# An RWKV-5 attention and SiLU feed-forward kernel: the first chunk's bonus term and state clearing move to ScalarE, and its y is finished one unit later

## The chip, the cores and the metric

The kernel runs on one core of a Trainium2 chip. Its engines are called as the profile calls them: PE (TensorE: matmuls; PEld is its weight load), DVE (VectorE), ACT (ScalarE), POOL (GpSimd) and SP (SyncE, which issues most DMAs). Each engine takes its instructions strictly in the order in which the program lists them, and waits at an instruction until all that it needs is there. The metric is the device time of one execution in microseconds (us), as the median of several runs.

## The reference

Four sequences of 768 tokens with 8 heads of 48 channels go through an RWKV-5 recurrence. Its result, 3072 tokens of 384 channels, goes through two matrices with a SiLU between them:

```
for t in range(768):
    cur   = outer(u * k[t], v[t])
    y[t]  = r[t] @ (state + cur)
    state = w * state + outer(k[t], v[t])
x   = y as (3072, 384)
h   = x @ w_in                      # 384 -> 2048
out = (h * sigmoid(h)) @ w_out      # 2048 -> 384
```

All inputs are float32. The state starts at zero.

## The kernel before

**Units.** Time is cut into 6 chunks of 128 tokens. A unit `i` is one chunk of one sequence: `divmod(i, 4)` gives chunk `sc` and sequence `b`, so units 0 to 3 are the first chunk of the four sequences, and there are 24. In a chunk the recurrence is written as matrix products: a masked 128x128 matrix A per head of decayed r and k times v (the part from inside the chunk), r times the state (the part from before; absent in chunk 0, where the state is zero), and the bonus term, which is the sum over channels of r\*u\*k, a number per token and head, times v.

**The steps of a unit** are small functions:
- `p1`: PE transposes r and k of the unit into PSUM (`tr`, `tk`); DVE multiplies them with the powers of the decay (`rT`, `kT`, lines 212 and 216). From unit 4 on ACT also makes a float16 copy of rT.
- `nat_v`: ACT casts v to float16. `nat_ku`, `nat_rk`: POOL computes k\*u and then r\*(k\*u). `nat_kc`: POOL computes k times the decay to the chunk's end (`kc`).
- `bonus_sum`: DVE sums r\*k\*u over the channels (`rku`, line 192). `bonus_vu`: POOL multiplies v by it (`vu`, line 198).
- `p2`: PE computes A of the even and odd heads (`ae`, `ao`, lines 226 and 228), DVE masks them to float16 (`am`, line 233).
- `p3y`: PE computes y from am, v and, from chunk 1 on, the state (lines 248, 251). `p3e`: DVE adds the bonus term and casts to float16 (`y16`, line 258).
- `p4`: PE transposes y16 (line 299), ACT copies it to SBUF (`xT`, line 300): the input of the feed-forward part.
- `sums`: PE computes the outer products of kc and v (line 267); `state`: DVE brings them into the state `st` and its float16 copy `st16` (lines 279, 281; 276 from chunk 1 on), and POOL scales the state for the next chunk (`sdec`).

The feed-forward part is cut into `l1(sc, ft)` (PE: x times 128 columns of `win`, line 311; ACT: SiLU, line 314) and `l2` (PE: times `wout`, line 323; DVE: copy out; SP: store). They stand in a list of fillers, from which `fill(n)` takes pieces to put between the steps of the attention part.

**Order.** The order of each engine is written out by hand. The program begins with the loads of six units on SP, constants, and a chain on DVE that builds the powers of the decay by doubling (`pi`, lines 148 to 152). Then comes the loop over units 0 to 3, in which no feed-forward work exists yet: there `spin(n)` issues n matmuls of zeros into a PSUM tile of its own. In round `s` the loop does p1, nat\_v, nat\_ku and nat\_rk of unit s, the bonus product, y, y16 and p4 of unit s-1, and p2 and bonus\_sum of unit s. Round 2 also issues the three loads of `win` on POOL's queue. After it come the loads of `wout` (POOL), k\*u and r\*k\*u of unit 4, kc of units 0 to 3, eight l1 for two sequences each, and p4 of unit 3 between them. Units 4 and 5 are then written out one step after another, with `sums` and `state` of units 0 to 5 among them; from unit 6 on there is a regular loop. A later load of a unit into one of the six input buffers waits until all who read the earlier unit there are done: for k that includes kc, for v it includes vu.

PSUM tiles share buffers by tag: `y` (two buffers) serves y, yT, sps, the row and column helpers and spin; `moe` (three) the l1 and l2 results and in the first loop tr and tk; `tA` (three) ae, ao and, later, tr and tk. A tile waits until its buffer is free.

Of the kernel before, what the change touches and what calls it, by code (L numbers as in the profile page):

```python
# [8 lines left out]
FP = mybir.dt.float32  # L9
F16 = mybir.dt.float16  # L10
AF = mybir.ActivationFunctionType
# [4 lines left out]
def kernel(  # L16
# [11 lines left out]
    nc = tc.nc  # L28

    B, H, S, D = r.shape  # L30
    C = 128
    NCH = S // C
    HD = H * D
    NP = H // 2
    PW = 2 * D
    PR = 64 + D
# [4 lines left out]
    NIN = 6  # L41
# [4 lines left out]
    wrk = ctx.enter_context(tc.tile_pool(name="wrk", bufs=2))  # L46
    ps = ctx.enter_context(tc.tile_pool(name="ps", bufs=1, space=bass.MemoryType.PSUM))
# [59 lines left out]
    nc.gpsimd.memset(pi[:, :, 0:1], 1.0)  # L107
    for i in range(NKC):
        nc.gpsimd.memset(kc[i][:, :, D:64], 0.0)
    for b in range(B):  # L110
        nc.gpsimd.memset(st[b], 0.0)
        nc.gpsimd.memset(st16[b], 0.0)
    for i in range(1, NIN):
        for t in (rin, kin):
            nc.vector.memset(t[i][:, :, D:64], 0.0)
    sil = cst.tile([128, 1], F16)
    nc.scalar.activation(out=sil, in_=junk[:, 0:1], func=AF.Silu)

    def spin(n):

        t = ps.tile([128, 512], FP, name="spin", tag="y", bufs=2)
        for _ in range(n):
            nc.tensor.matmul(t, junk[:, 0:128], junk, start=True, stop=True)

# [25 lines left out]
    n = 1  # L150
# [21 lines left out]
    def nat_ku(i):  # L172
        L = live.setdefault(i, {})
        L["ku"] = wrk.tile([128, H, D], FP, name="ku")
        nc.gpsimd.tensor_tensor(out=L["ku"], in0=kin[i % NIN][:, :, 0:D], in1=u_bc,  # L175
                                op=ALU.mult)

    def nat_rk(i):
        L = live[i]
        L["rku_f"] = wrk.tile([128, H, D], FP, name="rku_f")  # L180
        nc.gpsimd.tensor_tensor(out=L["rku_f"], in0=rin[i % NIN][:, :, 0:D], in1=L["ku"],  # L181
                                op=ALU.mult)

    def nat_kc(i):
        n = i % NIN
        nc.gpsimd.tensor_tensor(out=kc[i % NKC][:, :, 0:D], in0=kin[n][:, :, 0:D],  # L186
                                in1=lamC, op=ALU.mult)

    def bonus_sum(i):
        L = live[i]  # L190
        L["rku"] = wrk.tile([128, H], FP, name="rku")
        nc.vector.tensor_reduce(out=L["rku"], in_=L["rku_f"], axis=mybir.AxisListType.X,  # L192
                                op=ALU.add)

    def bonus_vu(i):
        L = live[i]
        L["vu"] = wrk.tile([128, H, D], FP, name="vu")
        nc.gpsimd.tensor_tensor(out=L["vu"], in0=vin[i % NIN],  # L198
                                in1=L["rku"].unsqueeze(2).broadcast_to([128, H, D]),
                                op=ALU.mult)  # L200

    def p1(i, tag="tA", mid=None):
        n = i % NIN
        L = live.setdefault(i, {})
        tr = ps.tile([128, NP, C], FP, name="tr", tag=tag, bufs=3)
        tk = ps.tile([128, NP, C], FP, name="tk", tag=tag, bufs=3)
        for t, src in ((tr, rin), (tk, kin)):
            flat = src[n].rearrange("p h d -> p (h d)")
            for p in range(NP):
                nc.tensor.transpose(t[0:PR, p, :], flat[:, 128 * p:128 * p + PR], ident)  # L210
        L["rT"] = wrk.tile([PR, NP, C], FP, name="rT")
        nc.vector.tensor_tensor(out=L["rT"], in0=tr[0:PR], in1=lamR, op=ALU.mult)  # L212
        if mid:
            mid()
        L["kT"] = wrk.tile([PR, NP, C], FP, name="kT")
        nc.vector.tensor_tensor(out=L["kT"], in0=tk[0:PR], in1=lamK, op=ALU.mult)  # L216
        if i >= B:
            L["rT16"] = wrk.tile([PR, NP, C], F16, name="rT16")
            nc.scalar.copy(out=L["rT16"], in_=L["rT"])  # L219

    def p2(i, between=None):
        L = live[i]
        ae = ps.tile([128, NP, C], FP, name="ae", tag="tA", bufs=3)
        ao = ps.tile([128, NP, C], FP, name="ao", tag="tA", bufs=3)
        for p in range(NP):
            nc.tensor.matmul(ae[:, p, :], L["kT"][0:D, p, :], L["rT"][0:D, p, :],  # L226
                             start=True, stop=True)
            nc.tensor.matmul(ao[:, p, :], L["kT"][64:PR, p, :], L["rT"][64:PR, p, :],  # L228
                             start=True, stop=True)
        L["am"] = []  # L230
        for a in (ae, ao):
            am = wrk.tile([128, NP, C], F16, name="am", bufs=4)
            nc.vector.tensor_tensor(out=am, in0=a,  # L233
                                    in1=maskM.unsqueeze(1).broadcast_to([128, NP, C]),
                                    op=ALU.mult)
            L["am"].append(am)
            if between:
                between()
                between = None

    def p3y(i):
        sc, b = unit(i)
        L = live[i]
        v16 = L["v16"]
        L["y"] = y = ps.tile([128, H, D], FP, name="y", tag="y", bufs=2)
        for p in range(NP):
            if sc:
                nc.tensor.matmul(y[:, 2 * p:2 * p + 2, :], L["rT16"][:, p, :],  # L248
                                 st16[b][:, p, :], start=True, stop=False)
            for j in range(2):  # L250
                nc.tensor.matmul(y[:, 2 * p + j, :], L["am"][j][:, p, :],  # L251
                                 v16[:, 2 * p + j, :], start=not sc,
                                 stop=(not sc or j == 1))

    def p3e(i):
        L = live[i]
        L["y16"] = wrk.tile([128, H, D], F16, name="y16")
        nc.vector.tensor_tensor(out=L["y16"], in0=L["y"], in1=L["vu"], op=ALU.add)  # L258
# [11 lines left out]
    def state(i):  # L270
        sc, b = unit(i)
        sps = live[i]["sps"]
        for p0, c0 in ((0, 0), (64, D)):
            dst = st[b][p0:p0 + D, :, c0:c0 + D]
            if sc:
                nc.vector.tensor_tensor(out=dst, in0=sps[p0:p0 + D, :, c0:c0 + D],
                                        in1=sdec[b][p0:p0 + D, :, c0:c0 + D], op=ALU.add)
            else:
                nc.vector.tensor_copy(out=st16[b][p0:p0 + D, :, c0:c0 + D],
                                      in_=sps[p0:p0 + D, :, c0:c0 + D])  # L280
                nc.vector.tensor_copy(out=dst, in_=sps[p0:p0 + D, :, c0:c0 + D])
        if sc:
            nc.gpsimd.tensor_copy(out=st16[b], in_=st[b])
        if sc < NCH - 2:
            nc.gpsimd.tensor_tensor(out=sdec[b], in0=st[b],
                                    in1=wCT.unsqueeze(2).broadcast_to([PR, NP, PW]),
                                    op=ALU.mult)
# [3 lines left out]
    def p4(i):  # L291
        sc, b = unit(i)
        L = live[i]
        if sc not in xts:
            xts[sc] = wrk.tile([128, NQ, B, C], F16, name="xT", bufs=3)
        yT = ps.tile([128, NQ, C], F16, name="yT", tag="y", bufs=2)
        yf = L["y16"].rearrange("p h d -> p (h d)")
        for q in range(NQ):
            nc.tensor.transpose(yT[:, q, :], yf[:, 128 * q:128 * q + 128], ident16)  # L299
        nc.scalar.copy(out=xts[sc][:, :, b, :], in_=yT)  # L300
# [48 lines left out]

    def to_cols_u():  # L350
        t = to_cols(urow)
        spin(1)
        to_rows(u_bc, lambda p: t[:, p:p + 1].broadcast_to([PR, 128]))

    for s in range(B):
        p1(s, tag="moe", mid=to_cols_u if s == 0 else None)
        nat_v(s)
        nat_ku(s)
        if s:
            bonus_vu(s - 1)  # L360
        nat_rk(s)
        if s == 2:
            for c0, c1 in ((0, 512), (512, 1024), (1024, 2048)):
                nc.gpsimd.dma_start(out=win[:, :, c0:c1],
                                    in_=moe_w_in[:, c0:c1]
                                    .rearrange("(q p) n -> p q n", p=128))
        if s:
            p3y(s - 1)
            p3e(s - 1)
        spin(3)  # L370
        p2(s)
        bonus_sum(s)
        spin(2)
        if s:
            p4(s - 1)
        if s == 1:
            to_rows(lamC, lambda p: lamCT[:, p, :])
        spin(2)
    bonus_vu(B - 1)
    p3y(B - 1)  # L380
    p3e(B - 1)
    nat_kc(0)
    for g in range(2):
        nc.gpsimd.dma_start(
            out=wout[:, 8 * g:8 * g + 8, :],
            in_=moe_w_out[1024 * g:1024 * g + 1024, :].rearrange("(f p) n -> p f n", p=128))
    a, b_ = B, B + 1
    nat_ku(a)
    nat_rk(a)
    for i in range(1, B):  # L390
        nat_kc(i)
    for ft in range(4):
        l1(0, ft, 0, 2)
    p4(B - 1)
# [12 lines left out]
    p1(a)  # L407
    fill(1)
    nat_v(a)
    bonus_sum(a)  # L410
    bonus_vu(a)
    sums(0)
    state(0)
    fill(1)
# [11 lines left out]
    sums(3)  # L426
    state(3)
    p1(b_)
    nat_ku(b_)
    nat_rk(b_)  # L430
    fill(1)
    p4(a)
    sums(a)
# [75 lines left out]
```

## Time and profile before

| | us |
|---|---|
| median of 10 runs | 219.46 (219.44 to 222.36) |
| profiled execution, its own time | 219.46 |
| its span, first to last instruction | 217.8 |
| PE busy | 207.0 |
| DVE busy | 118.5 |
| ACT busy | 92.7 |
| POOL busy | 118.9 |

The profile is one execution. Its span leaves out 1.66 us around the first and last instruction. PE is busy for 95% of it, but this counts the spin matmuls. The first l1 matmul starts at 26.15 us; the loop over units 0 to 3 runs before that. Idle time of an engine costs only where the engine that sets the end waits for it; the trace names, behind each wait, who ended it.

In timelines a line has the start and duration in us, the engine, the line of the kernel, the operation, what it writes and reads, its shape, a count and, in brackets, how long the engine was idle before it and what ended that. Several like instructions in a row stand as one line with their common duration. DMA runs at about 170 to 210 GB/s from 5 to 30 us and half of that in the middle of the kernel.

### The profile page before, as it was taken

Reading aid. Unit: us, or ns where it says so; the run is one execution under the profiler, and the core shown is the slowest. Engines: PE = TensorE matmul, PEld = TensorE weight load, DVE = VectorE, ACT = ScalarE, POOL = GpSimd, SP = SyncE. Lnnn points to the kernel's source line nnn. Section 1 sums busy time; section 2 is a strip of 40 time slices with the busy share of each in tenths; the row PEclk is TensorE's granted clock in tenths of the full one; section 3 lists DMA queues with packets and bytes.
Section 4 is the critical chain, followed back from the end, with each engine's and each line's share of the span. In section 5 each row is a group of like instructions: output and inputs, shape, how many; then the busy total and the mean of one; then the engine's idle time right before and its main releaser. Section 6 shows DMA issues by size and latency. Waiting matters only on the chain.

```text
span 217.8 us, 4605 instructions
## 1 busy us (share of the span) xinstructions
PE 207.0 (95%) x1781; PEld 137.3 (63%) x1781; DVE 118.5 (54%) x242; ACT 92.7 (43%) x192; POOL 118.9 (55%) x155
## 2 busy tenths in 40 slices
PE   7899988978999999999999999999999999999993
PEld 2566656557777787676567666567676557654561
DVE  6677749845385573586365467356466337520121
ACT  2403274556720572214783125782026772049400
POOL 8197699975744963948574675373475165200000
PEclk9999999999999999999999999999999999999999
DMA  4998999989943850738513465410210000110011
GB/s 93 206 210 171 191 197 186 194 176 192 188 92 89 186 107 3 180 81 178 108 39 73 116 140 123 93 39 2 75 38 36 3 0 22 55 72 0 3 72 72
DMA packets 81662, 22.32 MB, mean 103 GB/s; under 512 B 75368, under 2 KB 81256, under 8 KB 81640
## 3 DMA queue, kind: packets, MB, share of 16 engines
q1 hardware_dynamic: 78360, 18.88, 40.0%
q0 software_dynamic: 3280, 3.15, 9.0%
q8 instruction: 14, 0.23, 0.4%
q14 instruction: 8, 0.07, 0.1%
HBM read 20.45 MB, written 4.72 MB: 116 GB/s over the span
## 4 chain that ended last, share of the span: by engine, by line
PE 76%; POOL 6%; SPq 6%; DVE 5%; issue 2%; ACT 2%; DMA 2%; DVEq 0%; POOLq 0%
PE ops L323 29%; PE hps L311 24%; PE ae L226 9%; SPq L71 5%; PE tr L210 4%; PE tk L210 3%; PE sps L267 2%; DMA vin<-in_v_dram 2%; PE y L251 1%; PE yT L299 1%; PE y L248 1%; POOL rku_f L181 1%; DVE rT L212 1%; POOL vu L198 1%; DVE am L233 1%
## 5 line engine op out<-in xcount | busy, mean ns | idle before, releaser
L311 PE MATMUL hps<-xT,win 128*128 128x512 f16 (+1 forms) x348 | 70.5, 342 | 1.5 <-ACT gT L314 0.9
L323 PE MATMUL ops<-wout,gT 128*128 128x384 f16 x384 | 69.9, 326 | 0.0
L314 ACT ACTIVATE gT<-hps 128x512 f16<-128x512 f32 (+1 forms) x116 | 58.6, 524 | 24.0 <-PE hps L311 22.1
L198 POOL TENSOR_TENSOR vu<-vin,rku 128x384 f32<-128x384 f32 x24 | 19.9, 828 | 62.9 <-DVE rku L192 61.5
L323 PEld LDWEIGHTS <-gT 128*128 128x128 f16 x384 | 35.8, 98 | 21.3
L311 PEld LDWEIGHTS <-win 128*128 128x128 f16 x348 | 32.1, 98 | 24.1 <-issue 2.5
L233 DVE TENSOR_TENSOR am<-ae,maskM 128x512 f16<-128x512 f32 x24 | 16.6, 692 | 47.0 <-PE ao L228 47.0
L219 ACT CAST rT<-rT 112x512 f16<-112x512 f32 x20 | 12.4, 618 | 51.7 <-DVE rT L212 51.7
L327 DVE COPY osb<-ops 128x384 f32<-128x384 f32 x24 | 13.3, 556 | 33.2 <-PE ops L323 32.7
L226 PEld LDWEIGHTS ae<-rT,kT 48*128 48x128 f32 x192 | 23.1, 187 | 9.4 <-issue 6.7
L226 PE MATMUL ae<-rT,kT 48*128 48x128 f32 x192 | 27.7, 285 | 0.8 <-DVE kT L216 0.5
L228 PE MATMUL ao<-rT,kT 48*128 48x128 f32 x192 | 27.7, 285 | 0.0
L175 POOL TENSOR_TENSOR ku<-kin,u_bc 128x384 f32<-128x384 f32 x24 | 24.2, 1009 | 4.7 <-ACT u_bc L145 4.7
L181 POOL TENSOR_TENSOR rku_f<-rin,ku 128x384 f32<-128x384 f32 x24 | 24.0, 1001 | 1.6
L186 POOL TENSOR_TENSOR kc<-kin,lamC 128x384 f16<-128x384 f32 x24 | 23.9, 1000 | 0.0
L300 ACT COPY xT<-yT 128x384 f16<-128x384 f16 x24 | 11.4, 476 | 28.9 <-PE yT L299 28.9
L228 PEld LDWEIGHTS ao<-rT,kT 48*128 48x128 f32 x192 | 23.1, 187 | 0.0
L212 DVE TENSOR_TENSOR rT<-tr,pi 112x512 f32<-112x512 f32 x24 | 16.5, 689 | 9.0 <-PE tr L210 7.6
L233 DVE TENSOR_TENSOR am<-ao,maskM 128x512 f16<-128x512 f32 x24 | 16.4, 681 | 0.0
L216 DVE TENSOR_TENSOR kT<-tk,pi 112x512 f32<-112x512 f32 x24 | 16.3, 681 | 0.0
L258 DVE TENSOR_TENSOR y<-y,vu 128x384 f16<-128x384 f32 x24 | 13.3, 553 | 3.9 <-PE y L251 2.7
L210 PE MATMUL tr<-ident,rin 128*112 128x128 f32 x96 | 14.9, 279 | 0.0
(59 smaller groups left out, 208.8 us busy)
## 6 DMA issues: line engine op xcount, KB each, us to landing
rin<-in_r_dram SPq DMA_DIRECT2D x24, 192.0 KB, 4.0
kin<-in_k_dram SPq DMA_DIRECT2D x24, 192.0 KB, 3.6
vin<-in_v_dram SPq DMA_DIRECT2D x24, 192.0 KB, 3.6
out_dram<-osb SPq DMA_DIRECT2D x24, 192.0 KB, 1.9
wout<-in_moe_w_out_dram POOLq DMA_DIRECT2D x2, 768.0 KB, 12.5
win<-in_moe_w_in_dram POOLq DMA_DIRECT2D x2, 384.0 KB, 6.6
win<-in_moe_w_in_dram POOLq DMA_DIRECT2D x1, 768.0 KB, 10.0
wrow<-in_w_dram SPq DMA_DIRECT2D x1, 1.5 KB
```

Source lines behind the costliest of these rows:

```text
L175: nc.gpsimd.tensor_tensor(out=L["ku"], in0=kin[i % NIN][:, :, 0:D], in1=u_bc, op=ALU.mult)
L181: nc.gpsimd.tensor_tensor(out=L["rku_f"], in0=rin[i % NIN][:, :, 0:D], in1=L["ku"], op=ALU.mult)
L186: nc.gpsimd.tensor_tensor(out=kc[i % NKC][:, :, 0:D], in0=kin[n][:, :, 0:D], in1=lamC, op=ALU.mult)
L198: nc.gpsimd.tensor_tensor(out=L["vu"], in0=vin[i % NIN], in1=L["rku"].unsqueeze(2).broadcast_to([128, H, D]), op=ALU.mult)
L210: nc.tensor.transpose(t[0:PR, p, :], flat[:, 128 * p:128 * p + PR], ident)
L212: nc.vector.tensor_tensor(out=L["rT"], in0=tr[0:PR], in1=lamR, op=ALU.mult)
L226: nc.tensor.matmul(ae[:, p, :], L["kT"][0:D, p, :], L["rT"][0:D, p, :], start=True, stop=True)
L228: nc.tensor.matmul(ao[:, p, :], L["kT"][64:PR, p, :], L["rT"][64:PR, p, :], start=True, stop=True)
L233: nc.vector.tensor_tensor(out=am, in0=a, in1=maskM.unsqueeze(1).broadcast_to([128, NP, C]), op=ALU.mult)
L311: nc.tensor.matmul(hps, win[:, q, ft * 128:(ft + 1) * 128], xts[sc][:, q, b0:b1, :].rearrange("p b t -> p (b t)"), start=(q == 0), stop=(q ...
L314: nc.scalar.activation(out=gts[sc][:, ft, b0 * C:b1 * C], in_=hps, func=AF.Silu)
L323: nc.tensor.matmul(ops, gts[sc][:, ft, b * C:(b + 1) * C], wout[:, ft, :], start=(ft == 0), stop=(ft == NFT - 1))
```

## The change

Six edits, all for the units of the first chunk or for the steps just behind it:

1. POOL no longer zeroes the four states and their float16 copies at the start. A new function `clear` copies zeros with ACT, for states 0 and 1 at the end of round 0, for 2 and 3 at the end of round 1.
2. For units 0 to 3 the bonus product is made by ACT (`bonus_act`), one ACTIVATE per head with the sum as a scale per partition, in place of one POOL instruction. `rku` and `vu` get a third buffer.
3. Round s now does, of unit s-1, kc, bonus\_sum, the bonus product and y, and, of unit s-2, y16 (p3e) and p4. p3e stands ahead of p2 of the round. Round 3 also does bonus\_sum and the product of unit 3. y16 and p4 of units 2 and 3 follow the loop.
4. The spin matmuls write into the tile that the next real matmuls will fill (four ahead of the transposes, three ahead of ae), not into a tile of their own; `to_cols_u` has two in place of one. The rows of `lamC` are made in round 0, not in round 1.
5. In chunk 0 `state` makes the float16 copy on ACT; DVE keeps the float32 copy.
6. On POOL, k\*u and r\*k\*u of unit 5 and the bonus product of unit 4 stand ahead or beside the loads of `wout`; bonus\_sum(4) stands ahead of p1(4).

```diff
-    for b in range(B):
-        nc.gpsimd.memset(st[b], 0.0)
-        nc.gpsimd.memset(st16[b], 0.0)
...
+    def spin(n, t=None):
+        if t is None:
+            t = ps.tile([128, 512], FP, name="spin", tag="y", bufs=2)
+        else:
+            t = t.rearrange("s p t -> s (p t)")
...
+    def bonus_act(i):
+        L = live[i]
+        L["vu"] = wrk.tile([128, H, D], FP, name="vu", bufs=3)
+        for h in range(H):
+            nc.scalar.activation(out=L["vu"][:, h, :], in_=vin[i % NIN][:, h, :],
+                                 func=AF.Copy, scale=L["rku"][:, h:h + 1])
...
-    def p1(i, tag="tA", mid=None):
+    def p1(i, tag="tA", mid=None, spins=0):
...
+        spin(spins, tr)
...
-    def p2(i, between=None):
+    def p2(i, spins=0):
...
+        spin(spins, ae)
...
-                nc.vector.tensor_copy(out=st16[b][p0:p0 + D, :, c0:c0 + D],
-                                      in_=sps[p0:p0 + D, :, c0:c0 + D])
+                nc.scalar.copy(out=st16[b][p0:p0 + D, :, c0:c0 + D],
+                               in_=sps[p0:p0 + D, :, c0:c0 + D])
...
-        spin(1)
+        spin(2)
...
+    def clear(b):
+        zero = junk[0:PR, 0:HD].rearrange("r (p c) -> r p c", p=NP)
+        nc.scalar.copy(out=st[b], in_=zero)
+        nc.scalar.copy(out=st16[b], in_=zero)
+
     for s in range(B):
-        p1(s, tag="moe", mid=to_cols_u if s == 0 else None)
+        p1(s, tag="moe", mid=to_cols_u if s == 0 else None, spins=4 if s else 0)
         nat_v(s)
         nat_ku(s)
+        nat_rk(s)
         if s:
-            bonus_vu(s - 1)
-        nat_rk(s)
+            nat_kc(s - 1)
+            bonus_sum(s - 1)
+            bonus_act(s - 1)
+            p3y(s - 1)
+        if s == B - 1:
+            bonus_sum(s)
+            bonus_act(s)
         if s == 2:
             for c0, c1 in ((0, 512), (512, 1024), (1024, 2048)):
...
-        if s:
-            p3y(s - 1)
-            p3e(s - 1)
-        spin(3)
-        p2(s)
-        bonus_sum(s)
-        spin(2)
-        if s:
-            p4(s - 1)
-        if s == 1:
+        if s > 1:
+            p3e(s - 2)
+        p2(s, spins=3)
+        if s == 0:
             to_rows(lamC, lambda p: lamCT[:, p, :])
-        spin(2)
-    bonus_vu(B - 1)
+        if s > 1:
+            p4(s - 2)
+        if s < 2:
+            clear(2 * s)
+            clear(2 * s + 1)
+    p3e(B - 2)
     p3y(B - 1)
     p3e(B - 1)
-    nat_kc(0)
+    p4(B - 2)
+    a, b_ = B, B + 1
+    nat_ku(a)
+    nat_rk(a)
+    nat_kc(B - 1)
+    bonus_sum(a)
+    bonus_vu(a)
+    nat_ku(b_)
     for g in range(2):
...
-    a, b_ = B, B + 1
-    nat_ku(a)
-    nat_rk(a)
-    for i in range(1, B):
-        nat_kc(i)
+    nat_rk(b_)
...
-    bonus_sum(a)
-    bonus_vu(a)
...
-    nat_ku(b_)
-    nat_rk(b_)
```

More of the change, by code (lines that the diff above doesn't have):

```diff
@@ L117 @@
     nc.scalar.activation(out=sil, in_=junk[:, 0:1], func=AF.Silu)
-    def spin(n):
-        t = ps.tile([128, 512], FP, name="spin", tag="y", bufs=2)
+    def spin(n, t=None):
[3 more added lines that the diff above has]
+            t = t.rearrange("s p t -> s (p t)")
         for _ in range(n):
@@ L190, in bonus_sum @@
         L = live[i]
-        L["rku"] = wrk.tile([128, H], FP, name="rku")
+        L["rku"] = wrk.tile([128, H], FP, name="rku", bufs=3)
         nc.vector.tensor_reduce(out=L["rku"], in_=L["rku_f"], axis=mybir.AxisListType.X,
@@ L196, in bonus_vu @@
         L = live[i]
-        L["vu"] = wrk.tile([128, H, D], FP, name="vu")
+        L["vu"] = wrk.tile([128, H, D], FP, name="vu", bufs=3)
         nc.gpsimd.tensor_tensor(out=L["vu"], in0=vin[i % NIN],
@@ L200, in bonus_vu @@
                                 op=ALU.mult)
-    def p1(i, tag="tA", mid=None):
+    def bonus_act(i):
+        L = live[i]
+        L["vu"] = wrk.tile([128, H, D], FP, name="vu", bufs=3)
+        for h in range(H):
+            nc.scalar.activation(out=L["vu"][:, h, :], in_=vin[i % NIN][:, h, :],
+                                 func=AF.Copy, scale=L["rku"][:, h:h + 1])
+    def p1(i, tag="tA", mid=None, spins=0):
         n = i % NIN
@@ L236, in p2 @@
             L["am"].append(am)
-            if between:
-                between()
-                between = None
     def p3y(i):
```

## The prediction

> **What bounds the kernel now.** I read the page's busy shares first, then the table of windows, then TensorE's waits and timeline, and last the timelines of the other engines in the first 32 us. Shares, and four windows (us; busy time and instruction count of PE, PEld, DVE, ACT and POOL; granted clock; DMA share; GB/s):
>
> ```profile
> PE 207.0 (95%) x1781; PEld 137.3 (63%) x1781; DVE 118.5 (54%) x242; ACT 92.7 (43%) x192; POOL 118.9 (55%) x155
> ...
> 20.00:25.00 5.00, 4.88 (x53) 3.33 (x50) 3.88 (x7) 0.89 (x2) 4.38 (x6) 1.00 1.11 184
> 25.00:30.00 5.00, 3.99 (x40) 2.88 (x39) 1.92 (x4) 2.97 (x8) 3.55 (x5) 1.00 1.14 205
> 35.00:40.00 5.00, 4.04 (x44) 2.94 (x43) 4.85 (x15) 1.34 (x3) 4.56 (x6) 1.00 1.28 185
> 90.00:120.00 30.00, 30.00 (x271) 19.87 (x269) 17.57 (x34) 14.81 (x28) 19.24 (x24) 1.00 0.48 103
> ```
>
> From 60 to 200 us PE is full with work that the change leaves alone. So a microsecond won before 60 us comes off the end, and one lost is added. Up to 26 us PE looks busy, but much of that is spin matmuls; its first useful 256-column matmul (l1) starts at 26.15. After that it has short holes. From PE's timeline (start, duration, then in brackets the idle time before it and who ended it):
>
> ```profile
> 23.43 0.37 PE L226 MATMUL ae<-rT,kT 48*128 48x128 f32 x1
> ...
> 26.15 1.47 PE L311 MATMUL hps<-xT,win 128*128 128x256 f16 x12
> 27.92 0.34 PE L299 MATMUL yT<-ident,y 128*128 128x128 f16 x3 [0.30 <-DVE y L258]
> 28.83 1.36 PE L311 MATMUL hps<-xT,win 128*128 128x256 f16 x11 [0.57 <-ACT xT L300]
> 36.51 0.38 PE L267 MATMUL sps<-v,kc 128*112 128x96 f16 x4 [0.77 <-DVE st L281]
> 39.62 0.38 PE L267 MATMUL sps<-v,kc 128*112 128x96 f16 x4 [0.19 <-DVE st L281]
> 40.85 0.37 PE L226 MATMUL ae<-rT,kT 48*128 48x128 f32 x1 [0.21 <-DVE kT L216]
> 45.70 0.41 PE L267 MATMUL sps<-v,kc 128*112 128x96 f16 x4 [0.71 <-POOL kc L186]
> ```
>
> The question is therefore when that first l1, the second l1 group (28.83) and unit 5's ae (40.85) start afterwards. The rows that decide it, from the timelines of DVE, POOL and ACT:
>
> ```profile
> 3.99 1.60 DVE L148 COPY pi<-cols_sb 112x4 f32<-112x4 f32 x1
> 5.63 2.38 DVE L152 TENSOR_TENSOR pi<-pi 112x8 f32<-112x8 f32 x7
> ...
> 5.15 0.42 POOL L112 MEMSET stb<- 112x384 f16 x1
> 10.22 1.01 POOL L175 TENSOR_TENSOR ku<-kin,u_bc 128x384 f32<-128x384 f32 x1 [4.66 <-ACT u_bc L145]
> 19.14 2.47 POOL L364 DMA_DIRECT2D win<-in_moe_w_in_dram  x3
> ...
> 8.04 1.28 ACT L161 ACTIVATE lamCT<-pi 112x128 f32<-112x128 f32 x4 [5.74 <-DVE pi L152]
> ```
>
> **Zeroing leaves POOL.** Eight memsets go (2.66 to 5.57, 0.42 each). POOL has nothing to do then, so by themselves they are worth nothing. But the 112x4 copy L148 takes 1.60 us on DVE and ends 20 ns after the last memset, while an equal copy out of PSUM (L130) took 0.16. I take the memsets as its cause: the pi chain then ends at 6.6 instead of 8.0. The first rT moves from 8.15 to 6.9 (its transposes end at 6.85), kT from 8.82 to 8.0, because PE's u transposes at 7.63 set it, and u_bc's end from 10.14 to 9.35. The first ae comes at 9.4 instead of 10.20: 0.8 us earlier. If the copy stalls for another reason, this is 0. ACT pays with eight 112x384 copies at a pitch of 0.42 (v16: two in 0.93, one being 0.51), 1.7 us behind each of the first two units. That fits ACT's idle 5.33 us before 16.30.
>
> **Loop, units 0 to 2.** POOL does ku, rk, kc per unit (1.09 + 0.97 + 0.97, from pitches of those rows) instead of ku, vu, rk. Starting at 9.45 it ends kc(1) at 17.6. The three win triggers follow to 20.1 (19.14 to 21.61 before), then ku(3) and rk(3) to 22.15 (24.40 before). On DVE bonus_sum leaves its place between am and the next rT (0.46 of pitch, in the chain) for the place after kT, beside PE's 1.1 us of ae/ao. The chain per unit is then: ae/ao 1.1, am 1.3, transposes, rT and kT 1.3. The four spins ahead of the transposes hold the transposes back about as long as am takes (20.46 against 20.1 in unit 3), so putting spins inside awaited tiles is worth 0 to -0.4. By this count ae of units 1, 2, 3 starts at 13.8, 17.7, 21.8 (14.39, 19.23, 23.43 before): by unit 3 the loop is 1.6 us ahead. y16 was already beside ae/ao before (19.10, 23.48), so moving it gains nothing.
>
> **The bonus product on ACT.** One 0.83 us POOL instruction becomes eight ACTIVATEs of 128x48 with a pointer scale. No row has this shape. The nearest is lamCT (same function, pointer scale, 128 elements): four in 1.28 with 0.39 for one is a pitch of 0.297. The gT rows (0.598 for 512, 0.385 for 256) give 0.84 ns per element, so 48 elements are 0.23, and a product 1.85 us. Bounds: 0.12 (the 128x1 row, 0.21, less the overlap of 0.09) and 0.39 (no overlap). I take 0.23, nearest in kind.
>
> In units 1 and 2 this hides: product 0 runs 14.2 to 16.1, the zero copies of states 2 and 3 to 17.8, product 1 18.3 to 20.1, xT(0) to 20.5, and y(2) needs that PSUM buffer at 20.7. In unit 3 ACT must do two products in a row. rku(2) is ready at 22.2 and rku(3) at 22.7 (right behind POOL's rk(3)), so ACT is busy from 22.3 to 26.0, and xT(1) is queued behind: 26.0 to 26.45. On PE yT(2) waits for that PSUM buffer and l1 for xT(1), so the first l1 starts at 26.75, against 26.15: **0.6 later**, although its unit was 1.6 earlier. Behind it come xT(2), four gT (0.33 each) and xT(3), which ends at 29.2; the second l1 group starts at 29.25 against 28.83: **+0.4**. The 0.30 in front of yT(3) goes, and its gain is eaten by xT(3). bonus_sum(3) could hold am(3) behind it on DVE if POOL were late; by the count DVE is free at 22.15, just as rk(3) ends, and the cost is 0.2, included.
>
> **States 0 to 3 split over DVE and ACT.** DVE loses eight 48x192 copies (pitch 0.30), ACT gets them at about 0.32. kc(1) to kc(3), vu(4), ku(5) and rk(5) are now done on POOL before the first sums. Walking the same PE order from 29.25: sums(2) waits 0.3 instead of 0.77, sums(4) nothing instead of 0.19, and unit 5's kT is ready in time instead of 0.21 late; with the bonus_sum(4) ahead and the shorter DVE queue, ae(5) starts at 40.0, 0.85 ahead of 40.85. From the second l1 group to ae(5) it is then 10.75 us instead of 12.02: of these 1.27, 0.87 are the bracketed waits and 0.4 short gaps between PE's groups that carry no bracket. The 0.71 of kc(5) stays: am, rku, vu, kc follow ae(5) in the same order (4.85 us in both).
>
> **DMA.** win's triggers come 1.5 us earlier. Before, a piece took this long:
>
> ```profile
> DMA to landing us min/median/max: 6.1/7.1/10.0
> ```
>
> The first piece lands at 17.6 + 6.1 = 23.7. SP's loads of units 6 to 8 wait for kc and vu of units 0 to 2, so they now go out from about 19.7 instead of 28, and share the bus (about 190 GB/s). Sharing in halves would cost the 393 KB piece 2 us: 25.7, covered by PE's wait until 26.75; without that cover it adds its delay one for one. wout's triggers go from 28.17 to about 28.9 and are not needed before 57.
>
> **Sum.** +0.6 and +0.4 are one and the same delay seen twice, so: ae(5) 0.85 earlier, everything behind it unchanged, 219.46 - 0.85 = **218.6** (0.42 lost up to the second l1 group, 1.27 won behind it). The profiled execution's own time is 219.46 (span 217.8 and 1.66 around it), equal to the median.
>
> **Two rules of the skill.** PE's clock shows in the rows: four transposes took 1.06 us at 5.79 and 0.60 at 12.17. The Trainium skill (TensorE: Matmul & The Clock Gate, Part 1) says that an idle window of about 3.4 us halves the clock for the next one. By my count PE now has a hole from 23.4 to 26.5 with 0.2 us of work in it: under a window, so 0; if it fell in one, an estimate from that page is +1.7. The second: ScalarE: Activation LUTs, Rules for kernel authors, sends a multiplication to VectorE; its cost section (186 ns, 93 more for a pointer, 0.833 per element, 93 overlapped) gives 0.226 each, and the sum would still be 218.6.
>
> **Rivals.** *ACT is quick enough* (25%): at the low pitch of 0.12 xT(1) ends at 24.8, l1 starts at 25.5 behind y(3), the second group at 28.0: 217.3. For it: ACT was idle for 3.3 us of each unit before. Against: no row of ACT is that short. *No early start* (20%): the L148 stall is not POOL's; everything up to 26 us comes 0.8 later: 219.4, no change. Against it stands the 20 ns coincidence. *ACT's queue decides* (15%), the other side: a product is dearer than the count. At 0.297, as if length were free, three queued products push l1 to 27.8: 219.65; above about 0.29 the change no longer pays; at 0.39 product 1 also holds y(2) back, l1 starts at 30.35, and the time is 222.2. For it: 16 small instructions and xT(1) in one queue. *My forecast* holds 40%, 218.0 to 219.2.
>
> **How the numbers follow.** 0.5%, about what a measurement here can tell from no change, is 1.1 us: faster means below 218.36. Of my forecast a third lies there, of the quick ACT nearly all (0.13 + 0.24), and a little of the rest: 0.38. Slower (above 220.56) is most of the last rival: 0.14. Same is 0.48. The range runs from the quick ACT's 217.1 to 220.4, which leaves out the upper half of the ACT rival and a tail below.
>
> **What would show it.** Right: L148 near 0.15 us; first ae near 9.4 and fourth near 21.8; vu ACTIVATEs with a pitch of 0.23; a PE hole of about 3 us ahead of the first l1, ended by ACT xT; sums(2) waiting 0.3 or less. Wrong: L148 still 1.6; vu pitch of 0.3 or more; l1 ended by win's DMA; l2 or PE's transposes at half speed after 26 us.

## The result and the profile after

The changed kernel takes 221.08 us (median of 15 runs, 219.95 to 222.20) against 219.46 before. The ratio is 1.0059 with a 95% interval of 1.0037 to 1.0081: slower by about 0.6%, where 218.6 had been forecast. (The ratio and its interval are taken over all runs and not from the medians.) The single times fall into groups by the TensorE clock that the record of each run shows: 2 of 15 runs have a granted clock of 1.000 (219.95 and 220.09), 9 have 0.989 to 0.992 (about 221), 4 have 0.981 to 0.983 (about 222.1). The profiled execution is one of the middle group, 221.09 us with a span of 219.4.

First the table of windows of the changed kernel (columns as before: us, then busy time and count of PE, PEld, DVE, ACT and POOL, granted clock, DMA share, GB/s):

```profile
20.00:25.00 5.00, 3.01 (x41) 1.94 (x40) 4.22 (x8) 3.58 (x16) 4.84 (x6) 1.00 1.20 191
25.00:30.00 5.00, 3.60 (x21) 2.65 (x21) 1.02 (x2) 3.13 (x9) 3.83 (x5) 0.66 1.14 208
```

Two things differ from before. In 20 to 25 us PE was busy 4.88 us, now 3.01: the hole that the forecast expected. And the next row has a granted clock of 0.66, where every row of the kernel before had 1.00. The record of the clock gives its limits: half speed from 25.45 for 3.41 us, full speed from 28.86.

PE's timeline shows what that costs:

```profile
8.79 0.37 PE L235 MATMUL ae<-rT,kT 48*128 48x128 f32 x1
...
21.23 0.37 PE L235 MATMUL ae<-rT,kT 48*128 48x128 f32 x1
...
22.62 0.34 PE L305 MATMUL yT<-ident,y 128*128 128x128 f16 x3 [0.23 <-DVE y L264]
24.28 0.37 PE L257 MATMUL y<-v,am 128*128 128x48 f16 x8 [1.32 <-DVE y L264]
25.80 0.48 PE L305 MATMUL yT<-ident,y 128*128 128x128 f16 x3 [1.15 <-ACT xT L306]
26.07 2.76 PE L317 MATMUL hps<-xT,win 128*128 128x256 f16 x12
...
29.68 1.47 PE L317 MATMUL hps<-xT,win 128*128 128x256 f16 x12 [0.60 <-ACT xT L306]
...
37.66 0.38 PE L273 MATMUL sps<-v,kc 128*112 128x96 f16 x4 [0.60 <-DVE st L287]
41.26 0.38 PE L273 MATMUL sps<-v,kc 128*112 128x96 f16 x4 [0.68 <-DVE st L287]
42.48 0.37 PE L235 MATMUL ae<-rT,kT 48*128 48x128 f32 x1 [0.21 <-DVE kT L224]
```

The first l1 starts at 26.07, as before (26.15), although ae of unit 3 was 2.2 us earlier (21.23 against 23.43). Its twelve matmuls then take 2.76 us, where the same twelve took 1.47: the half clock. The second group starts at 29.68 instead of 28.83. From there to ae(5) it is 12.80 us, 0.78 more than before (12.02), and 2.05 more than the forecast's 10.75. The waits for `st` in front of sums, which were to shrink, are 0.60 and 0.68.

DVE's timeline tells why:

```profile
3.98 0.17 DVE L148 COPY pi<-cols_sb 112x4 f32<-112x4 f32 x1
...
34.11 0.35 DVE L287 COPY st<-sps 48x192 f32<-48x192 f32 x1 [1.19 <-ACT stb L285]
34.83 0.36 DVE L287 COPY st<-sps 48x192 f32<-48x192 f32 x1 [0.38 <-ACT stb L285]
```

And ACT's, for the same state and for the bonus products:

```profile
21.67 3.72 ACT L206 ACTIVATE vu<-vin,rku 128x48 f32<-128x48 f32 x16 [1.43 <-DVE rku L192]
25.29 0.46 ACT L306 COPY xT<-yT 128x384 f16<-128x384 f16 x1
...
33.76 0.31 ACT L285 CAST stb<-sps 48x192 f16<-48x192 f32 x1
34.49 0.31 ACT L285 CAST stb<-sps 48x192 f16<-48x192 f32 x1 [0.41 <-DVE st L287]
```

ACT (33.76), DVE (34.11), ACT (34.49), DVE (34.83): the two engines take turns, each released by the other, so a state takes 1.43 us. Two copies on one engine take 0.74 (a run below), so two engines side by side would need about that; this is an estimate. Both read the same PSUM tile. The first turn has a second part: DVE was free at 32.91, and ACT came to its copy only at 33.76, behind other work in its queue, so most of DVE's 1.19 us is ACT's queue.

### The profile page after: what moved, and what is told of

It is laid out like the page before. It is cut to its first block, busy times and chain, and to the rows that moved or that the text cites. A ratio compares the mean times of both kernels' runs of the same rounds, so it can differ in the third digit from the quotient of the medians.

```text
span 219.4 us, 4606 instructions
## 1 busy us (share of the span) xinstructions
PE 206.4 (94%) x1778; PEld 137.1 (63%) x1778; DVE 115.0 (52%) x234; ACT 105.7 (48%) x240; POOL 113.2 (52%) x143
## 4 chain that ended last, share of the span: by engine, by line
PE 82%; DVE 8%; ACT 6%; issue 1%; POOL 1%; DVEq 0%; ACTq 0%
PE ops L329 29%; PE hps L317 25%; PE ae L235 11%; PE tr L218 4%; PE tk L218 3%; DVE rT L220 2%; PE yT L305 2%; ACT vu L206 2%; PE sps L273 2%; PE y L257 2%; PE y L254 1%; PE tr L123 1%; DVE kT L224 1%; DVE am L242 1%; ACT rT L227 1%
## 5 line engine op out<-in xcount | busy, mean ns | idle before, releaser
L317 PE MATMUL hps<-xT,win 128*128 128x512 f16 (+1 forms) x348 | 71.8, 347 | 1.5 <-ACT gT L320 0.9
L198 POOL TENSOR_TENSOR vu<-vin,rku 128x384 f32<-128x384 f32 x20 | 16.6, 828 | 61.3 <-DVE rku L192 60.1
L317 PEld LDWEIGHTS <-win 128*128 128x128 f16 x348 | 32.7, 100 | 24.6 <-issue 2.5
L291 POOL TENSOR_TENSOR sdec<-st,pi 112x384 f32<-112x384 f32 x16 | 13.3, 834 | 6.6 <-DVE st L287 6.6
```

The lines of the kernel that those rows point to most:

```text
L198: nc.gpsimd.tensor_tensor(out=L["vu"], in0=vin[i % NIN], in1=L["rku"].unsqueeze(2).broadcast_to([128, H, D]), op=ALU.mult)
L317: nc.tensor.matmul(hps, win[:, q, ft * 128:(ft + 1) * 128], xts[sc][:, q, b0:b1, :].rearrange("p b t -> p (b t)"), start=(q == 0), stop=(q ...
```

## The experiments

The theory after the first reading: at full clock the change is worth almost nothing, because what the loop wins, the states lose; the hole on PE then costs a window of half clock in most runs. The rivals: ACT's queue is simply too full for the states; the half clock is a mark and not a cause; the gain from the start of the kernel was never there. Each ratio below is to the kernel before, run beside it on the same chip, where its median was 219.48 or 219.49. The kernel before has runs at 221.0 to 222.4 too (12 of 50, 5 of 29, 7 of 19 and 1 of 8 in the four series; with clocks of 0.984 to 0.992 in the last three), and they count in the ratio; so a ratio can lie under 1 where the median lies above.

| run | median us | ratio (95%) | runs under clock 0.995 |
|---|---|---|---|
| states' copies back on DVE | 220.25 | 1.0018 (0.9993 to 1.0043) | 7 of 10 |
| spins in the hole, 6 and 5 | 219.70 | 0.9994 (0.9971 to 1.0017) | 0 of 10 |
| float16 states from SBUF | 218.81 | 0.9951 (0.9923 to 0.9978) | 7 of 10 |
| zeroing on ACT alone | 218.19 | 0.9932 (0.9907 to 0.9957) | 0 of 8 |
| states from SBUF, spins 6 and 5 | 217.63 | 0.9906 (0.9874 to 0.9937) | 0 of 5 |
| states from SBUF, product 3 on POOL | 216.13 | 0.9839 (0.9804 to 0.9874) | 0 of 4 |
| the same, 6 spins | 216.20 | 0.9840 (0.9805 to 0.9875) | 0 of 4 |
| the same, 2 spins per unit fewer | 216.08 | 0.9838 (0.9802 to 0.9873) | 0 of 4 |
| spins in the hole, 6 and 0 | 219.71 | 0.9975 (0.9938 to 1.0012) | 0 of 10 |
| spins in the hole, 2 and 2 | 219.72 | 0.9983 (0.9950 to 1.0017) | 0 of 10 |

### The float16 copies of the states back on DVE

```diff
-                nc.scalar.copy(out=st16[b][p0:p0 + D, :, c0:c0 + D],
-                               in_=sps[p0:p0 + D, :, c0:c0 + D])
+                nc.vector.tensor_copy(out=st16[b][p0:p0 + D, :, c0:c0 + D],
+                                      in_=sps[p0:p0 + D, :, c0:c0 + D])
```

> The changed kernel, with the float16 state copies of chunk 0 back on DVE (edit 5 undone alone). Theory A, in the trace of the changed kernel ACT's st16 copy and DVE's st copy out of the same PSUM tile wait for each other in turn, so that a state takes 1.43 us: undone, the second l1 group to ae(5) takes the 12.0 us of the kernel before, not 12.8, and the median goes from 221.08 to about 220.3. Theory B, the copies are late only because ACT's queue (SiLU, v16) is in front of them: the same 220.3 here, it is told apart by the run with ACT reading SBUF. Rival C, the states do not matter and all of the loss is the half clock at 25.5 to 28.9 us: stays at 221.1.

220.25, as theories A and B both have it: 0.83 less than the changed kernel. Its profiled execution happens to have full clock, with the second l1 group at 28.61 and ae(5) at 40.53, 11.92 us apart. So edit 5 cost 0.9 us in that stretch (12.81 with it at full clock), and the other edits bring 0.1 there (12.02 before), where the forecast had 1.27 for all of them. Rival C falls.

### The float16 states made from SBUF

```diff
-                nc.scalar.copy(out=st16[b][p0:p0 + D, :, c0:c0 + D],
-                               in_=sps[p0:p0 + D, :, c0:c0 + D])
                 nc.vector.tensor_copy(out=dst, in_=sps[p0:p0 + D, :, c0:c0 + D])
+                nc.scalar.copy(out=st16[b][p0:p0 + D, :, c0:c0 + D], in_=dst)
```

> The changed kernel with ACT making the float16 states from DVE's float32 copy in SBUF, not from PSUM; DVE copies first. Theory A (two engines on one PSUM tile take turns): DVE does both copies of a state in 0.6 us right behind sums, sums(2) waits 0.3 or less, the stretch from the second l1 group to ae(5) falls from 12.8 to about 10.8 us and the median from 221.08 to 219.1 (half clock window still there). Theory B (ACT's queue is too late): y(4) and y(5) then wait for the states and the median stays within 0.5 of 221.1. Rival C (states do not matter): 221.1.

218.81, 2.27 less than the changed kernel. ACT has as many copies as in the changed kernel, in the same queue; it only reads another memory. DVE now does both halves in one go, and ACT follows. DVE and then ACT in this run:

```profile
32.78 0.74 DVE L285 COPY st<-sps 48x192 f32<-48x192 f32 x2
```

```profile
33.64 0.72 ACT L286 CAST stb<-st 48x192 f16<-48x192 f32 x2
```

No wait of PE's sums for a state is left, although ACT comes to its copy no earlier (33.64 against 33.76). So theory B falls as it was put: nobody waits for ACT's copies as such. The cost was that DVE and ACT had to read one PSUM tile in turn. How much of it is the turns and how much is ACT's queue, which DVE stood behind in its turn, this run does not split, since it also lets DVE go first; DVE first with both reading PSUM was not tried. The turns are kept by semaphores in the program, as the waits show; whether the chip would allow the two reads at once was not tried. The Trainium skill names a reason for turns (PSUM — Partial Sum Buffer, PSUM bank collisions raise a hardware error): no two engines may touch one bank and quadrant of PSUM at the same time, ACT and DVE reading included, so such accesses are guarded. Its further remark, that different quadrants (32 partitions each) of a bank may be read at once, is shown by no run here; by it ACT's second copy, from partition 64 on, need not have waited 0.41 us for DVE's first, of partitions 0 to 47.

### Spins in the hole

```diff
+    def warm(n):
+        spin(n, ps.tile([128, NP, C], FP, name="warm", tag="tA", bufs=3))
     p3e(B - 2)
+    warm(6)
     p3y(B - 1)
     p3e(B - 1)
+    warm(5)
     p4(B - 2)
```

> The changed kernel with 6 spin matmuls ahead of y(3) and 5 ahead of yT(2), into a PSUM buffer that nobody needs then, so that PE is not idle from 22.9 to 25.8 us. Theory, the hole makes the clock gate halve PE's clock for one window of 3.41 us, which costs up to 1.3 us in the l1 group (2.76 us for 12 matmuls, 1.47 before): granted clock 1.00 in every run, median 220.0, like the runs of the changed kernel that had clock 1.00 (219.95 and 220.09). Rival, the half clock is only a mark of something else (the group was waiting for win's DMA or for ACT): about 221 again, l1 group still over 2 us.

All ten runs lie between 219.68 and 220.03 with a clock of 0.996 or more; the median is 219.70, 1.38 less than the changed kernel. PE's timeline of this run:

```profile
22.79 1.46 PE L123 MATMUL warm<-junk 128*128 128x512 f16 x6
24.27 0.37 PE L257 MATMUL y<-v,am 128*128 128x48 f16 x8
24.49 1.24 PE L123 MATMUL warm<-junk 128*128 128x512 f16 x5
...
25.96 1.50 PE L317 MATMUL hps<-xT,win 128*128 128x256 f16 x12
...
28.30 1.47 PE L317 MATMUL hps<-xT,win 128*128 128x256 f16 x12 [0.67 <-ACT xT L306]
```

Useless matmuls that start nothing sooner take 1.4 us off: the first l1 still begins at 25.96, when xT(1) is there, but its group takes 1.50 and not 2.76. The half clock is the cause and not a mark. Without it the second group starts 0.53 earlier than before (28.30 against 28.83), and the states give back 0.79, which is about the whole difference of 0.2 us to the kernel before. The expected median was 220.0, that of the two full-clock runs without spins; the 0.3 between are no part of the hole (see the start of the kernel, below).

Two weaker doses ask how much work the clock needs. Six spins ahead of y(3) alone:

> The changed kernel with 6 spins ahead of y(3) and none ahead of yT(2): the second part of the hole, 1.15 us, stays. Theory, what halves the clock is a window of 3.41 us that is mostly idle, and not idle time as such: the window ahead of the half clock was busy for 1.06 us in the changed kernel and is now busy for about 2.3 us, so the clock stays at 0.996 or more and the median is 219.7. Rival, any gap of 1 us does it: 0.99 in most runs and about 221.

And two in each part:

> The changed kernel with 2 spins in either part of the hole, so that the window is busy for about 1.9 of its 3.41 us. If the gate asks for about half of the window (it fell after windows busy for 1.06 and 1.54 us, and stayed up where the least busy one had 2.05 us), the clock stays at 0.996 or more and the median is 219.7 to 220.0; if it asks for more than that, most runs are at 0.99 and the median is near 221.

219.71 and 219.72, with a clock of 0.996 or more in all twenty runs. So four spins in place of eleven are enough, and a gap of 1.15 us by itself does nothing. What precedes a half-speed window is a window of the same 3.41 us with little work in it. In all twelve profiles every stretch of full clock is a whole multiple of 3.41 us long (20.48 and 191.15 us in the changed kernel, 6 and 56 windows), so the limits of the windows can be counted from any change of the clock. The windows ahead of the half clock in the profiled executions, first of the changed kernel:

```profile
22.04:25.45 3.41, 1.06 (x19) 0.62 (x16) 2.21 (x6) 3.41 (x16) 3.28 (x4) 1.00 1.21 198
```

and of the one with states from SBUF, where the half clock began at 27.03:

```profile
23.62:27.03 3.41, 1.54 (x20) 1.33 (x21) 1.68 (x4) 2.99 (x13) 2.24 (x3) 1.00 1.18 199
```

PE was busy for 31% and 45% of them. The run with the states' copies back on DVE has the same hole, and its profiled execution has full clock. There the limits, counted from 7.03 us, cut the hole in two, and neither window was followed by half speed:

```profile
20.68:24.10 3.42, 2.26 (x27) 1.28 (x22) 3.42 (x8) 2.13 (x10) 3.27 (x4) 1.00 1.18 183
24.10:27.51 3.41, 1.79 (x23) 1.54 (x24) 1.43 (x3) 2.99 (x13) 2.24 (x3) 1.00 1.18 201
```

These are 66% and 52%. With two spins in each part the emptiest window after the start, 23.90 to 27.31 in that profile, has 2.12 us (62%). As far as PE's busy time decides, the limit thus lies between 45% and 52% of a window. The windows start at another time of the kernel in each execution, and that also explains why the changed kernel's runs differ: the same hole is caught by one window, by two, or by none. No execution with two was profiled, but the granted clocks fit: a half-speed window takes 0.008 off the mean of a span of 219.4 us, two take 0.016.

### Zeroing by ACT alone, in the kernel before

```diff
-    for b in range(B):
-        nc.gpsimd.memset(st[b], 0.0)
-        nc.gpsimd.memset(st16[b], 0.0)
...
         bonus_sum(s)
         spin(2)
+        if s < 2:
+            clear(2 * s)
+            clear(2 * s + 1)
```

> The kernel before with edit 1 alone: states zeroed by ACT in rounds 0 and 1, not by POOL at the start. Theory: the 112x4 copy on DVE at 3.99 us falls from 1.60 to 0.17 us since no POOL memset runs beside it; the first rT comes at 6.8 (8.15), POOL's first ku near 8.9 (10.22), and the first l1 near 25.2 (26.15): 218.3 to 218.7. Rival: the copy still falls, but the loop over units 0 to 3 is bound by something later (POOL behind win's triggers, u, spins), and the time stays at 219.4.

218.19, 1.3 us (0.7%) less than the kernel before, from one edit out of six. DVE's timeline has the copy, PE's the first ae:

```profile
3.99 0.17 DVE L145 COPY pi<-cols_sb 112x4 f32<-112x4 f32 x1
```

```profile
9.39 0.37 PE L223 MATMUL ae<-rT,kT 48*128 48x128 f32 x1
```

1.60 us became 0.17, and the loop, untouched, ends earlier: in this execution the first ae comes 0.81 us sooner (10.20 before) and so does the first l1 (25.34 against 26.15). The profiled execution took 218.74 and is one of two that are only 0.75 to 0.78 faster than the kernel before; the other six took 218.16 to 218.20. A likely reason is in the section on the prediction. The copy waits while POOL's memsets run, which agrees with the Trainium skill (GPSIMD Engine Reference, Key points): POOL shares its SBUF interfaces with VectorE, and VectorE instructions of certain kinds contend with it.

### Both cures together

The edits of the runs with SBUF states and with 6 and 5 spins, in one kernel.

> The changed kernel with both cures: 6 and 5 spins in the hole ahead of the first l1, and ACT's float16 states made from SBUF. Theory, the two losses are separate and add: the hole's cure is worth 1.38 (221.08 to 219.70), the states' cure 2.05 at full clock (about 220.0 to 217.96): 217.65, clock 0.998 or more in every run. Rival, they overlap (a state that is ready sooner is only waited for because the clock was low): 218.3 or more.

217.63, spread 0.03 us. The two losses are separate and add: 219.70 less 2.07, where the states' cure alone gave 2.05 at full clock. The clock was 0.996 or more, where 0.998 had been expected. The difference between 221.08 and this is that of the two cures.

### One product back on POOL

```diff
-        if s:
-            nat_kc(s - 1)
+        if s and s < B - 1:
+            nat_kc(s - 1)
+        if s:
             bonus_sum(s - 1)
             bonus_act(s - 1)
             p3y(s - 1)
         if s == B - 1:
             bonus_sum(s)
-            bonus_act(s)
+            bonus_vu(s)
+            nat_kc(s - 1)
```

with the states from SBUF as above.

> The changed kernel with ACT's float16 states made from SBUF and with the bonus product of unit 3 alone back on POOL, right behind r*k*u of unit 3, so that ACT has one product and not two ahead of xT(1). Theory, the two products in one queue set the first l1: xT(1) ends 1.8 us earlier, near 24.0 us, the hole on PE shrinks to 1.4 us, the first l1 comes near 24.7 (26.07), the second group near 27.3, and the median is 216.9, nearly always at full clock. Rival, POOL pays it back: kc(2), kc(3) and ku(4) come 0.8 us later and sums or unit 4 wait: 217.9.

216.13, 1.5% faster than the kernel before and the best of all but for a tie. ACT and PE:

```profile
21.67 1.91 ACT L206 ACTIVATE vu<-vin,rku 128x48 f32<-128x48 f32 x8 [1.43 <-DVE rku L192]
23.48 0.46 ACT L305 COPY xT<-yT 128x384 f16<-128x384 f16 x1
```

```profile
23.99 0.36 PE L257 MATMUL y<-v,am 128*128 128x48 f16 x8 [1.04 <-ACT xT L305]
24.27 0.34 PE L304 MATMUL yT<-ident,y 128*128 128x128 f16 x3
24.45 1.50 PE L316 MATMUL hps<-xT,win 128*128 128x256 f16 x12
26.80 1.47 PE L316 MATMUL hps<-xT,win 128*128 128x256 f16 x12 [0.67 <-ACT xT L305]
37.54 0.37 PE L235 MATMUL ae<-rT,kT 48*128 48x128 f32 x1
```

xT(1) comes 1.81 us sooner (23.48 against 25.29), the second l1 group 1.50 sooner than with the spins, and POOL pays nothing back. The gain of 1.8 us, measured from the full-clock runs with SBUF states alone (217.95 to 218.02), beat the 1.05 expected, because yT(2) is no longer held either and the group's first half follows y(3) directly. From the second group to ae(5) it is 10.74 us. What is left of the hole, 1.04 us, does not disturb the clock in four runs.

Six spins in that rest:

> The same with 6 spins in what is left of the hole, ahead of y(3). Theory: nothing is left for the clock gate, the runs agree within 0.3 us at 216.6 to 216.9. Rival, the spins run past am(3) and delay y(3): 0.2 to 0.4 slower than without them.

216.20, the same: there is nothing left to cure, and nothing is lost. And with two spins in place of four ahead of each unit's transposes:

> The same again with two spins instead of four ahead of the transposes of units 1 to 3. Theory, the four spins hold the transposes back (DVE is idle 0.55, 0.1 and 0.29 us ahead of rT in the changed kernel): 0.6 to 0.9 us faster than with four, near 216.0. Rival, PE is then too idle for the clock gate in the loop and some runs drop to a clock of 0.99: 217 or more.

216.08, again the same; 0.6 to 0.9 less had been expected, a miss. DVE's timeline shows where the time went, in front of the second of the two bonus sums of round 3:

```profile
21.88 0.55 DVE L192 TENSOR_REDUCE rku<-rku_f 128x8 f32<-128x384 f32 x1 [0.88 <-POOL rku_f L181]
```

The transposes are earlier, and DVE then waits 0.88 us for POOL's r\*k\*u of unit 3, behind the triggers of win. This execution is the slowest of its four (216.47), and POOL's product starts 0.42 us later in it than in the run before (20.85 against 20.43); so about half of the wait is this execution's own, an estimate. The rest of the wait says that POOL is the bound at this point of the loop.

## Why the prediction was wrong

**The clock gate, +1.38 us, is the step that turned the sign.** The forecast saw the hole (23.4 to 26.5 by its count, 22.96 to 25.80 in fact) and had the rule in hand, but priced it at 0 because the hole was shorter than a window of 3.4 us. That reads "idle" as "without any work". The runs show that a window busy for 31% or 45% already halves the clock of the next. The Trainium skill's page (TensorE: Matmul & The Clock Gate, Part 1) states the window's length rightly, 3.41 us measured; its "idle window" is not to be taken literally. The price named for that case, +1.7, was near the 1.38 measured (221.08 to 219.70; the two profiled executions have their full clock from 4.97 and 5.74 us, which makes no difference to the first ae); only its chance was wrong: it was no case among the rivals, and happened in 13 of 15 runs.

**The states, +2.06 us, are the second.** The step "states 0 to 3 split over DVE and ACT" put the stretch from the second l1 group to ae(5) at 10.75 us; it measured 12.81 at full clock. The forecast took for granted that two engines copy out of one PSUM tile side by side. They take turns, and DVE stands behind ACT's queue in them, so the split made a state slower (1.43 us) than DVE alone (1.26 in the run with the copies back on DVE). With the tile read by one engine only, the stretch is 10.74 us (28.30 to 39.04 with both cures). That this hits 10.75 is in part luck: sums(2) does not wait at all there, where 0.3 had been counted.

**The start was better than forecast, by 0.95, and more than half of that is the clock.** The copy L148 went to 0.17 as forecast. The term for it was 0.8, and at the same start of the clock it was right: where PE's clock is full only from 7.54 us (zeroing on ACT alone; 7.59 in the profile before), the first ae comes at 9.39, where 9.4 was forecast. But the start differs between executions. In the profiles the first ae of the changed kernel and its variants comes at 8.78 or 8.79 where the clock is full by 6.01 us, and at 8.86, 8.99, 9.09 and 9.20 where it is full from 6.55, 6.83, 7.03 and 7.26. So the u transposes, which the forecast had taken as fixed at 7.63, came at 6.36 in the changed kernel (full from 4.97), and the gain was 1.4. The kernel before does not show it in its usual runs, which agree within 0.1 us; there, the first rT and kT come only behind the slow copy. The start also fits the 0.2 to 0.4 us between runs of one kernel at full clock, such as 219.70 and 219.95: two profiled executions with spins, at 219.70 and 219.91, have their first ae at 8.79 and 8.99. For the runs that were not profiled this is an inference. The lead stays: the fourth ae came at 21.23, not 21.8. ACT's two products then started at 21.67, not 22.3, so xT(1) ended at 25.75, not 26.45, and at full clock the second l1 group came at 28.30, not 29.25.

**These three make up the error:** 218.6 + 1.38 + 2.06 - 0.95 = 221.09. The last two are read from one trace, that with spins, so that they add up is no proof; each of the two losses is shown by the run that takes it away.

**The bonus product was right**, in size and in place: eight in 1.91 us, a pitch of 0.227 against 0.23, sixteen in 3.72 right behind rku(2), and xT(1) behind them, which held yT(2) and the first l1. The l1 itself came at 26.07 (25.96 with spins), not at 26.75, by the better start. The run with one product on POOL shows it as a cause: 1.50 us. The estimate from the cost section of the Trainium skill's page (ScalarE: Activation LUTs) was 0.226.

**DMA** did not matter, as forecast: win's triggers moved from 19.14 to 16.86, and no wait of the first two l1 groups is put down to a piece.

**The rivals.** "No early start" is refuted by the run of that edit alone. "ACT is quick enough" did not occur, since ACT's queue did set the first l1. "ACT's queue decides" named the right queue, but with a pitch that was not there. The mechanism that made the kernel slower stood in a sentence on the clock without a chance of its own.

## What to carry to other kernels

A gap on TensorE is priced by the busy share of a whole clock window (3.41 us here), not by the length of the gap: where a window can fall to 45% or less, fill it, even with matmuls of zeros, or the next window may run at half speed. Work moved to a second engine cost 0.9 us here, where both engines had to read one PSUM tile; letting one engine empty PSUM and the other read its copy in SBUF gave 2.05. And before six edits are judged together, run the suspect ones alone: here one gave -1.3 us, another took 0.9 of it back, and a gap on PE 1.4; with two small repairs the sum became 3.3 us faster than the kernel before.

## What the hardware showed beyond that

A 112x4 copy on VectorE took 1.60 us while POOL ran memsets of 0.42 us each into other tiles, and 0.17 without them: eight memsets that nobody waited for cost the kernel 1.3 us in the median. TensorE's half-speed windows last 3.41 us and start at another time of the kernel in each execution, so a kernel with one hole of this kind has times in steps of about 1.1 us (219.95, 221, 222.1), and one without it repeats to 0.03 us in the best case. The kernel before has such runs too (5 of 29 in one series, at 221.1, clock 0.992). Their cause stays open: none was profiled, and in its profiled execution no window from 7.59 to 205 us is busy for less than 2.53 us.
